# Windowed attention into a squared-ReLU MLP on one core: from a scheduler's order to the written order, with rows 0 and 1 laid out by hand

## The chip, the core and the metric

The kernel runs on one core of a Trainium2 chip. The metric is the device time of one execution in microseconds (us). The engines are TensorE (PE in the profile; PEld is its weight load), VectorE (DVE), ScalarE (ACT), GpSimd (POOL) and SyncE (SP, which here only issues DMAs).

## The reference

Attention over 8 batch rows, 8 heads, 576 positions and head size 64 is followed by a two-layer product. Heads 0 to 3 see a plain window of 32 positions, heads 4 to 7 every fourth position in a window of 128.

```
scores = matmul(q, k^T) / sqrt(64)          # (8, 8, 576, 576)
plain:   0 <= i - j < 32
dilated: 0 <= i - j < 128 and (i - j) % 4 == 0
attn = softmax(where(mask, scores, -1e9)); o = matmul(attn, v)
x = o as (4608 tokens, 512)                 # token = row * 576 + position
out = (max(x @ w_in, 0) ** 2) @ w_out       # w_in (512, 2048), w_out (2048, 512)
```

## The kernel before

The kernel works in fp16 with fp32 sums. A row is one batch index. The 4608 tokens are also cut into nine chunks of 512 for the two products. Chunk c needs rows up to c, so chunk b-1 is worked beside the attention of row b.

**Loads.** SP issues the loads of sliding q and k into `sq` (L83), of v into `sv` in six pieces (L92) and of dilated v into `sd` in two (L97, L98). These three buffers exist once. POOL issues the casting loads: dilated q and k into `nd` (L105), `w_in` into `wi` in three pieces (L110), `w_out` into `wo` in four quarters (L117). Stores of the output go out on SP too (L232). A row loads 1.18 MB into `sq`, 0.75 into `sv`, 0.82 into `sd` and 0.59 into `nd`.

**Casts.** `cast_sliding_qk` makes `nq` from `sq` in four pieces, two of q and two of k: in row 0 on ACT (q) and DVE (k), later on POOL. `cast_v_sliding` and `cast_v_dilated` make `vp` and `vd` from `sv` and `sd` on POOL.

**Attention of a row.** PE transposes q and k into PSUM (`pt`, `pd`), and DVE and ACT copy them to `QKTp` and `QKTd`. PE forms score tiles (`ps`, `pz`), ACT takes their exponential into `AT` (L288), DVE multiplies by the 0/1 mask (L289). PE forms values and row sums (`pav`, `paw`), DVE normalizes them into `x` (L330, L331), PE transposes them back (`px`, `py`), and DVE copies that into `xT` (L380, L398), which is the input of the first product. All these PSUM tiles share a pool of two buffers of two banks, `papool`: each tile waits until the one two places earlier has been read out.

**The two products of a chunk** are a generator, `moe_gen`. For each of 16 `ffc`, four matmuls sum `ph` (L205), ACT applies the ReLU into `rt` (L215; three buffers), and DVE squares it into `g` (L216). Then for each of four token tiles `t`, 16 matmuls sum `po` (L221), ACT copies it to `ot` (L231; three buffers), and SP stores it. `ph` and `po` share a pool of four PSUM buffers, `pmool`. One step of the generator is two matmuls. `pump(n)` takes n steps, and `attn` calls it with a `gap` between the steps of attention.

**Who sets the order.** The kernel is written in one sequence, and the framework's scheduler then orders each engine's instructions by priority, moving ready work ahead of what was written before it. So the built order isn't the written one. Three one-column writes to `sq`, `sv` and `sd` (L451 to L453) stand in the source after the first product's beginning, but on DVE they are built into row 0's opening, ahead of the masks and inside the mask multiplications. Row 1's loads depend on them and are issued right behind row 0's. In row 1 and later the second score tile of a pair (`ps_0_1`) was placed two `ph` matmuls behind the first (`ps_0_0`).

Of the kernel before, what the change touches and what calls it, by code (L numbers as in the profile page):

```python
# [8 lines left out]
FP16 = mybir.dt.float16  # L9
# [4 lines left out]
P = 128  # L14
# [3 lines left out]
def kernel(  # L18
# [43 lines left out]
    pmool = ctx.enter_context(tc.tile_pool(name="pmool", bufs=4, space=bass.MemoryType.PSUM))  # L62


    xT = const.tile([P, NDM, NTOK], FP16, name="xT")
    wi = wpool.tile([P, NDM, DFF], FP16, name="wi")
    wo = wpool.tile([P, NFF, DM], FP16, name="wo")
# [29 lines left out]
        nc.sync.dma_start(out=sd[PADD:P, 0, :, :], in_=vv[0:QD])  # L97
        nc.sync.dma_start(out=sd[:, 1, :, :], in_=vv[QD - PADD : CL])  # L98

    def load_dilated_qk(b):  # L100
        nd = natp.tile([QB, 2, 2, 12 * D], FP16, name=f"nd{b}", tag="nd")
        for i, src in enumerate((q, k)):
            s4 = src[b, HH:H].rearrange("(g e) (p j) d -> e p g (j d)", e=2, j=12)
            for e in range(2):
                nc.gpsimd.dma_start(out=nd[48 * e : 48 * (e + 1), i, :, :], in_=s4[e])  # L105
        return nd

    def load_w_in():
        for f0, f1 in ((0, 512), (512, 1024), (1024, 2048)):
            nc.gpsimd.dma_start(  # L110
                out=wi[:, :, f0:f1],
                in_=moe_w_in[:, f0:f1].rearrange("(dh dl) f -> dl dh f", dl=P),
            )
# [17 lines left out]
    def cast_sliding_qk(b, engs):  # L131
        n = natp.tile([QB, 2, 6, HH, D], FP16, name=f"nq{b}", tag="nq")
        for i in range(2):
            for half in range(2):
                j0 = 3 * half
                copy(
                    engs[i],
                    n[:, i, j0 : j0 + 3, :, :],
                    sq[:, i, :, D * j0 : D * (j0 + 3)].rearrange("p h (j d) -> p j h d", d=D),
                )  # L140
        return n

    def cast_v_sliding():
        for m in range(0, NB, 2):
            nc.gpsimd.tensor_copy(vp[:, m : m + 2, :, 0:D], sv[:, m : m + 2, :, :])  # L145
# [8 lines left out]


    load_sliding_qk(0)
    nds = {0: load_dilated_qk(0)}
    nc.vector.memset(sv[0:PADP, 0, :, :], 0.0)
    nc.vector.memset(sd[0:64, 0, :, :], 0.0)
    load_v(0)  # L160
# [2 lines left out]
    nc.scalar.activation(warm, warm, ACTF.Exp)  # L163

    make_identity(nc, ident)
    reli = const.tile([P, QB], I16, name="reli")
    nc.gpsimd.iota(reli, pattern=[[1, QB]], base=0, channel_multiplier=-1)
    relf = const.tile([P, QB], FP32, name="relf")
    nc.vector.tensor_copy(relf, reli)
    lo_ = const.tile([P, QB], FP16, name="lo_")  # L170
# [26 lines left out]
    )  # L197


    def moe_gen(c):  # L200
        g = gp.tile([P, NFF, TOKC], FP16, name=f"g{c}", tag="g")
        for ffc in range(NFF):
            ph = pmool.tile([P, TOKC], FP32, name=f"ph{c}_{ffc}", tag="pm")
            for dmk in range(NDM):
                nc.tensor.matmul(  # L205
                    ph,
                    wi[:, dmk, ffc * P : ffc * P + P],
                    xT[:, dmk, c * TOKC : (c + 1) * TOKC],
                    start=(dmk == 0),
                    stop=(dmk == NDM - 1),  # L210
                )
                if dmk == 1:
                    yield
            rt = osb.tile([P, TOKC], FP16, name=f"rt{c}_{ffc}", tag="rt")
            nc.scalar.activation(rt, ph[:], ACTF.Relu)  # L215
            nc.vector.tensor_mul(g[:, ffc, :], rt, rt)  # L216
            yield
        for t in range(TOKC // P):
            po = pmool.tile([P, DM], FP32, name=f"po{c}_{t}", tag="pm")
            for ffc in range(NFF):  # L220
                nc.tensor.matmul(  # L221
                    po,
                    g[:, ffc, t * P : (t + 1) * P],
                    wo[:, ffc, :],
                    start=(ffc == 0),
                    stop=(ffc == NFF - 1),
                )
                if ffc % 2 == 1 and ffc < NFF - 1:
                    yield
            ot = osb.tile([P, DM], FP32, name=f"ot{c}_{t}", tag="ot")  # L230
            nc.scalar.copy(ot, po)  # L231
            nc.sync.dma_start(  # L232
                out=out[(c * 4 + t) * P : (c * 4 + t + 1) * P, :], in_=ot
            )
            yield

    pending: list = []

    def pump(n):
        for _ in range(n):  # L240
            while pending:
                try:
                    next(pending[0])
                    break
                except StopIteration:
                    pending.pop(0)
# [5 lines left out]
    def t_sliding(b, n, hp):  # L252
        pt = pa(f"pt{b}_{hp}", FP16)
        for i in (1, 0):
            for j in range(6):
                nc.tensor.transpose(  # L256
                    pt[:, i, QB * j : QB * (j + 1)],
                    n[:, i, j, 2 * hp : 2 * hp + 2, :],
                    ident[0:QB, 0:QB],
                )  # L260
        for i, eng in ((1, nc.vector), (0, nc.scalar)):
            copy(
                eng,
                QKTp[:, i, hp, PADP:].rearrange("x (p j) -> x p j", j=6),
                pt[:, i, 0:UW].rearrange("x (j p) -> x p j", j=6),
            )
# [101 lines left out]
    def x_sliding(b, half, xs):  # L368
        px = pa(f"px{b}_{half}", FP16)
        for m3 in range(3):  # L370
            m = 3 * half + m3
            x = xs[m // 2][:, m % 2].rearrange("p h d -> p (h d)")
            for c in range(2):
                nc.tensor.transpose(
                    px[:, 0, 288 * c + QB * m3 : 288 * c + QB * (m3 + 1)],
                    x[:, P * c : P * (c + 1)],
                    ident[0:QB, 0:QB],
                )
        t0 = b * S + 288 * half
        nc.vector.tensor_copy(  # L380
            xT[:, 0:2, t0 : t0 + 288],
            px[:, 0, 0:UW].rearrange("x (c t) -> x c t", c=2),
        )

    def x_dilated(b, t, xs):
        py = pa(f"py{b}_{t}", FP16)
        for a in range(2):
            for e in range(2):
                x = xs[a][:, e].rearrange("p h d -> p (h d)")
                for c in range(2):  # L390
                    o = 288 * c + QD * (2 * a + e)
                    nc.tensor.transpose(  # L392
                        py[:, 0, o : o + QD],
                        x[0:QD, P * c : P * (c + 1)],
                        ident[0:QD, 0:QD],
                    )
        t0 = b * S + 288 * t
        nc.vector.tensor_copy(  # L398
            xT[:, 2:4, t0 : t0 + 288].rearrange("x c (i r) -> x c i r", r=DIL),
            py[:, 0, 0:UW].rearrange("x (c r i) -> x c i r", c=2, r=DIL),  # L400
        )

    def attn(b, nq, nd, gap):
        t_sliding(b, nq, 0)
        pump(gap)
        t_sliding(b, nq, 1)
        pump(gap)
        t_dilated(b, nd, 0)
        pump(gap)
        s_sliding(b, 0)  # L410
        pump(gap)
        t_dilated(b, nd, 1)
        pump(gap)
        s_sliding(b, 1)
        pump(gap + 2)
        s_dilated(b, 0)
        pump(gap + 2)
        s_dilated(b, 1)
        pump(gap + 1)
        xs = []  # L420
        for mp in range(3):
            xs.append(av_sliding(b, mp))
            pump(gap)
            if mp == 1:
                x_sliding(b, 0, xs)
                pump(gap)
        ys = []
        for a in range(2):
            ys.append(av_dilated(b, 0, a))
            pump(gap)  # L430
        x_sliding(b, 1, xs)
        pump(gap)
        zs = []
        for a in range(2):
            zs.append(av_dilated(b, 1, a))
            pump(gap)
        x_dilated(b, 0, ys)
        pump(gap)
        x_dilated(b, 1, zs)

    nq = cast_sliding_qk(0, (nc.scalar, nc.vector))
    cast_v_sliding()
    load_w_in()
    cast_v_dilated()
    load_w_out()
    attn(0, nq, nds[0], 0)
    pending.append(moe_gen(0))
    pump(1)
    pump(14)

    nc.vector.memset(sq[:, :, :, 0:1], 0.0)  # L451
    nc.vector.memset(sv[:, 1, :, 0:1], 0.0)
    nc.vector.memset(sd[:, 1, :, 0:1], 0.0)  # L453
    load_sliding_qk(1)
    load_v(1)
    nds[1] = load_dilated_qk(1)
    pump(18)
    for b in range(1, B):
        if b > 1:
            pending.append(moe_gen(b - 1))  # L460
            pump(1)
        nq = cast_sliding_qk(b, (nc.gpsimd, nc.gpsimd))
        cast_v_sliding()
        cast_v_dilated()
        if b + 1 < B:
            load_sliding_qk(b + 1)
            load_v(b + 1)
            nds[b + 1] = load_dilated_qk(b + 1)
        attn(b, nq, nds[b], 1 if b == 1 else 3)
        pump(1000)  # L470
    for c in range(B - 1, NTOKC):
        pending.append(moe_gen(c))
# [31 lines left out]
```

## Time and profile before

| | |
|---|---|
| times of three runs | 356.32, 1806.59, 355.76 us; median 356.32 |
| profiled execution | 355.09 us, span of its trace 353.3 us, TensorE clock 0.99 |
| busy in the span | PE 318.3, DVE 192.2, ACT 158.9, POOL 83.2 us |
| matmuls L205 and L221 | 576 each, 64 in a row take 13.8 us |
| DMA | 40.81 MB moved |

The span runs from the first instruction to the last; the profiled execution's own time is 1.8 us longer. PE's busy time counts modelled ends of pipelined matmuls, so single matmuls look longer (0.38 us) than their pitch (0.216 us). Idle time of an engine other than PE costs nothing by itself; it matters where PE waits for it.

### The profile page before, as it was taken

The numbers are of one execution on the slowest core, as the hardware profiler recorded it, in microseconds if no ns is written. First come the engines' busy times: TensorE is split into PE (matmuls) and PEld (weight loads), VectorE is DVE, ScalarE is ACT, GpSimd is POOL, SyncE is SP. The second block draws the span as 40 slices with busy tenths as digits, with TensorE's granted clock in tenths as the row PEclk, the third lists the DMA queues.
The fourth block names the chain that finished last, engine by engine and source line by source line (L and its number), as shares of the span: only waits on it lengthen the run. The fifth ranks groups of instructions, "written<-read, shape, count | busy, mean of one in ns | idle before, by whom it ended". The sixth has DMA issues, their size and how long they took to land.

```text
span 353.3 us, 6704 instructions
## 1 busy us (share of the span) xinstructions
PE 318.3 (90%) x2656; PEld 164.3 (46%) x2656; DVE 192.2 (54%) x422; ACT 158.9 (45%) x296; POOL 83.2 (24%) x130
## 2 busy tenths in 40 slices
PE   0468875996999999999999999999999999999995
PEld 0355332553455545554555455545554554444442
DVE  2676951764874576557655775577557653402400
ACT  3250641605931594149414941494149415614611
POOL 3471527057252322232223222002200000000000
PEclk9999996999999999999999999999999999999999
DMA  8999999959994482448243424300110011011011
GB/s 183 224 211 202 208 254 194 207 131 258 248 196 129 141 170 58 129 128 188 58 125 118 67 58 129 115 2 3 61 60 0 2 68 52 0 61 59 1 61 60
DMA packets 49840, 40.81 MB, mean 116 GB/s; under 512 B 26000, under 2 KB 44688, under 8 KB 49808
## 3 DMA queue, kind: packets, MB, share of 16 engines
q1 hardware_dynamic: 42528, 31.46, 35.1%
q0 software_dynamic: 7280, 8.92, 15.0%
q8 instruction: 21, 0.34, 0.4%
q14 instruction: 11, 0.09, 0.1%
HBM read 39.85 MB, written 9.44 MB: 139 GB/s over the span
## 4 chain that ended last, share of the span: by engine, by line
PE 61%; DMA 16%; ACT 7%; DVE 6%; issue 4%; POOL 2%; SPq 2%; POOLq 0%; ACTq 0%
PE po L221 31%; PE ph L205 22%; DMA sq<-in_k_dram 5%; DMA wi<-in_moe_w_in_dram 4%; DMA sq<-in_q_dram 3%; ACT rt L215 3%; DVE QKTd L129 3%; DVE g L216 2%; DMA sv<-in_v_dram 2%; SPq L92 2%; PE paw L359 2%; DMA out_dram<-ot 2%; ACT QKTd L127 1%; PE pt L256 1%; POOL nq L129 1%
## 5 line engine op out<-in xcount | busy, mean ns | idle before, releaser
L205 PE MATMUL ph<-xT,wi 128*128 128x512 f16 x576 | 139.1, 382 | 2.3 <-ACT rt L215 1.0
L221 PE MATMUL po<-wo,g 128*128 128x512 f16 x576 | 140.1, 381 | 0.0
L215 ACT ACTIVATE rt<-ph 128x512 f16<-128x512 f32 x144 | 84.9, 608 | 36.2 <-PE ph L205 32.8
L216 DVE TENSOR_TENSOR g<-rt 128x512 f16<-128x512 f16 x144 | 68.7, 480 | 58.5 <-ACT rt L215 56.0
L205 PEld LDWEIGHTS <-wi 128*128 128x128 f16 x576 | 51.6, 98 | 57.5 <-issue 3.7
L231 ACT COPY ot<-po 128x512 f32<-128x512 f32 x36 | 21.1, 586 | 121.4 <-PE po L221 110.7
L221 PEld LDWEIGHTS <-g 128*128 128x128 f16 x576 | 51.4, 98 | 50.2 <-issue 0.6
L129 POOL CAST nq<-sq 96x768 f16<-96x768 f32 x28 | 24.1, 894 | 43.3 <-PE pt L256 20.7
L145 POOL CAST vp<-sv 128x512 f16<-128x512 f32 x24 | 16.3, 682 | 74.3 <-PE pav L345 35.3
L150 POOL CAST vd<-sd 128x512 f16<-128x512 f32 x32 | 19.5, 624 | 32.9 <-PE paw L359 25.6
L288 ACT ACTIVATE AT<-ps 128x576 f16<-128x576 f32 x32 | 19.8, 671 | 11.2 <-PE ps L298 11.2
L331 DVE TENSOR_TENSOR x_d<-paw,rcp_d 72x512 f16<-72x512 f32 x32 | 22.0, 686 | 1.1
L272 PE MATMUL pd<-ident,nd 96*128 96x96 f16 x192 | 12.1, 219 | 10.2 <-DMA nd<-in_k_dram 6.8
L256 PE MATMUL pt<-ident,nq 96*128 96x96 f16 x192 | 11.7, 215 | 10.1 <-DVE nq L129 9.6
L129 DVE COPY QKTp<-pt 128x576 f16<-128x576 f16 x16 | 12.0, 756 | 14.1 <-PE pt L256 14.1
L288 ACT ACTIVATE AT<-pz 128x576 f16<-128x576 f32 x32 | 19.1, 650 | 0.1
L289 DVE TENSOR_TENSOR AT<-AT,maskp 128x576 f16<-128x576 f16 x32 | 15.0, 468 | 7.5 <-ACT AT L288 5.1
L129 DVE COPY QKTd<-pd 128x288 f16<-128x288 f16 x32 | 13.0, 448 | 9.2 <-PE pd L272 9.1
L272 PEld LDWEIGHTS <-nd 96*128 96x128 f16 x192 | 11.1, 105 | 14.0 <-issue 10.9
L398 DVE COPY xT<-py 128x576 f16<-128x576 f16 x16 | 12.1, 757 | 9.9 <-PE py L392 9.9
L256 PEld LDWEIGHTS <-nq 96*128 96x128 f16 x192 | 10.6, 103 | 13.6 <-DVE nq L129 9.6
L289 DVE TENSOR_TENSOR AT<-AT,maskd 128x576 f16<-128x576 f16 x32 | 15.1, 474 | 3.2 <-ACT AT L288 0.3
(51 smaller groups left out, 194.5 us busy)
## 6 DMA issues: line engine op xcount, KB each, us to landing
out_dram<-ot SPq DMA_DIRECT2D x36, 256.0 KB, 2.4
sv<-in_v_dram SPq DMA_DIRECT2D x40, 128.0 KB, 4.4
sq<-in_q_dram SPq DMA_DIRECT2D x8, 576.0 KB, 10.5
sq<-in_k_dram SPq DMA_DIRECT2D x8, 576.0 KB
sd<-in_v_dram SPq DMA_DIRECT2D x8, 512.0 KB
nd<-in_q_dram POOLq DMA_DIRECT2D x16, 144.0 KB, 5.8
nd<-in_k_dram POOLq DMA_DIRECT2D x16, 144.0 KB, 6.0
sd<-in_v_dram SPq DMA_DIRECT2D x8, 288.0 KB
```

Source lines behind the costliest of these rows:

```text
L129: eng.tensor_copy(o, i)
L150: nc.gpsimd.tensor_copy(vd[:, t, c : c + 2, :, 0:D], sd[:, t, :, D * c : D * (c + 2)].rearrange("p h (c d) -> p c h d", d=D),)
L205: nc.tensor.matmul(ph, wi[:, dmk, ffc * P : ffc * P + P], xT[:, dmk, c * TOKC : (c + 1) * TOKC], start=(dmk == 0), stop=(dmk == NDM - 1),)
L215: nc.scalar.activation(rt, ph[:], ACTF.Relu)
L216: nc.vector.tensor_mul(g[:, ffc, :], rt, rt)
L221: nc.tensor.matmul(po, g[:, ffc, t * P : (t + 1) * P], wo[:, ffc, :], start=(ffc == 0), stop=(ffc == NFF - 1),)
L231: nc.scalar.copy(ot, po)
L256: nc.tensor.transpose(pt[:, i, QB * j : QB * (j + 1)], n[:, i, j, 2 * hp : 2 * hp + 2, :], ident[0:QB, 0:QB],)
L272: nc.tensor.transpose(pt[:, i, QB * j : QB * (j + 1)], n[:, i, g, P * j : P * (j + 1)], ident[0:QB, 0:QB],)
L288: nc.scalar.activation(AT[:, u, 0:UW], ps[:, :, 0 : UW // 2], ACTF.Exp, scale=scale)
L289: nc.vector.tensor_mul(AT[:, u, 0:UW], AT[:, u, 0:UW], mask)
L331: nc.vector.tensor_tensor(out=x[0:w], in0=pv[:, :, :, 0:D], in1=rcp[0:w].unsqueeze(3).to_broadcast([w, 2, HH, D]), op=ALU.mult,)
```

## The change

The kernel enters `tc.manual_schedule()`, and from there each engine follows the order in which the code is written. The code is laid out anew for it:

- Row 0: the index pattern `reli` is made on POOL ahead of the `nd` loads; the masks come ahead of the k cast on DVE; q is cast by ACT, the first half of k by DVE, the second by POOL; `w_in` is issued after that cast and ahead of the v casts. Attention of row 0 stands alone, without products between its steps.
- The first product of chunk 0 follows. After three of its 16 `ffc`, DVE writes one column of `sq` and of row 1's `nd` buffer; row 1's `sq` and `nd` loads depend on these writes, and `w_out` is issued after them. `sv` and `sd` of row 1 are written and loaded after row 1's first transposes.
- The second product of chunk 0 goes by quarters of `w_out`, with four `po` sums open at a time (`mm2_by_rows_gen`). Row 1's attention is laid between its steps.
- `xT` copies (L380, L398) are on ACT in all rows.
- In rows 2 to 7 `pav_2` comes ahead of `px_0`, and gaps are 3 and 4 steps in the scores, and 3 in the values (2 in row 2, which begins with 12 steps of the first product).

In the order built from it, each engine has the same kinds of instructions as before, apart from the 32 `xT` copies that went from DVE to ACT, a second one-column write, and the k cast of row 0. In a later row DVE's sequence is now first `QKTp` copy, `g_0`, `g_1`, second `QKTp` copy, `g_2`, `QKTd` copies, `g_3`; before it was first `QKTp` copy, `g_0`, second `QKTp` copy, `g_1`, `g_2`, `QKTd` copies, `g_3`. ACT's is now first `QKTp` copy, `rt_0`, `rt_1`, second `QKTp` copy, `rt_2`, `QKTd` copies, `rt_3`; before it was `rt_0`, first `QKTp` copy, `rt_1`, second `QKTp` copy, `rt_2`, `rt_3`, `QKTd` copies. `ps_0_1` follows `ps_0_0` on PE directly.

```diff
+    ctx.enter_context(tc.manual_schedule())
...
     load_sliding_qk(0)
-    nds = {0: load_dilated_qk(0)}
+    reli = const.tile([P, QB], I16, name="reli")
+    nc.gpsimd.iota(reli, pattern=[[1, QB]], base=0, channel_multiplier=-1)
+    nds = {0: dilated_buffer(0)}
+    load_dilated_qk(0, nds[0])
...
+    def mm2_by_rows_gen(c, g):
+
+        pos = [
+            pmool.tile([P, DM], FP32, name=f"po{c}_{t}", tag="pm") for t in range(TOKC // P)
+        ]
+        for f4 in range(0, NFF, 4):
+            for t, po in enumerate(pos):
+                for ffc in range(f4, f4 + 4):
+                    mm2(c, g, po, t, ffc)
+                    if ffc % 2 == 1 and ffc < NFF - 1:
+                        yield
+                if f4 + 4 == NFF:
+                    store(c, t, po)
+                    yield
...
-        nc.vector.tensor_copy(
+        nc.scalar.copy(
             xT[:, 0:2, t0 : t0 + 288],
...
-        nc.vector.tensor_copy(
+        nc.scalar.copy(
             xT[:, 2:4, t0 : t0 + 288].rearrange("x c (i r) -> x c i r", r=DIL),
...
-    nq = cast_sliding_qk(0, (nc.scalar, nc.vector))
+    nq = cast_sliding_qk(0, (nc.scalar, nc.scalar, nc.vector, nc.gpsimd))
+    load_w_in()
     cast_v_sliding()
-    load_w_in()
     cast_v_dilated()
+    attn_scores(0, nq, nds[0], (0, 0))
+    attn_values(0, 0)
+    g0 = hidden(0)
+    pending.append(mm1_gen(0, g0))
+    pump(6)
+    nds[1] = dilated_buffer(1)
+    nc.vector.memset(sq[:, :, :, 0:1], 0.0)
+    nc.vector.memset(nds[1][:, :, :, 0:1], 0.0)
+    load_sliding_qk(1)
+    load_dilated_qk(1, nds[1])
     load_w_out()
-    attn(0, nq, nds[0], 0)
-    pending.append(moe_gen(0))
-    pump(1)
-    pump(14)
-
-    nc.vector.memset(sq[:, :, :, 0:1], 0.0)
+    nq = cast_sliding_qk(1, (nc.gpsimd,) * 4)
+    pump(26)
+    pending.append(mm2_by_rows_gen(0, g0))
+    t_sliding(1, nq, 0)
     nc.vector.memset(sv[:, 1, :, 0:1], 0.0)
     nc.vector.memset(sd[:, 1, :, 0:1], 0.0)
-    load_sliding_qk(1)
     load_v(1)
-    nds[1] = load_dilated_qk(1)
-    pump(18)
-    for b in range(1, B):
-        if b > 1:
-            pending.append(moe_gen(b - 1))
-            pump(1)
-        nq = cast_sliding_qk(b, (nc.gpsimd, nc.gpsimd))
+    cast_v_sliding()
+    cast_v_dilated()
+    load_sliding_qk(2)
+    load_v(2)
+    nds[2] = dilated_buffer(2)
+    load_dilated_qk(2, nds[2])
+    pump(2)
+    attn_scores(1, nq, nds[1], (2, 2), begun=True)
+    attn_values(1, 1)
+    pump(1000)
+    for b in range(2, B):
+        pending.append(moe_gen(b - 1))
+        pump(12 if b == 2 else 1)
+        nq = cast_sliding_qk(b, (nc.gpsimd,) * 4)
...
-        attn(b, nq, nds[b], 1 if b == 1 else 3)
+        attn_scores(b, nq, nds[b], (3, 4))
+        attn_values(b, 2 if b == 2 else 3)
         pump(1000)
```

## The prediction

> **What bounds the kernel now.** I read the page's busy times first, then the table by stretches cut at row boundaries, then the timeline of the two stretches where TensorE (PE) stands still, then one steady row engine by engine.
>
> ```profile
> PE 318.3 (90%) x2656; PEld 164.3 (46%) x2656; DVE 192.2 (54%) x422; ACT 158.9 (45%) x296; POOL 83.2 (24%) x130
> ...
> q1 hardware_dynamic: 42528, 31.46, 35.1%
> q0 software_dynamic: 7280, 8.92, 15.0%
> ```
>
> PE is the bound. The queues give prices: q1 took 0.351 x 353.3 = 124 us for 31.46 MB, 3.9 us per MB; the casting queue q0 took 53 us for 8.92 MB, 5.9 us per MB.
>
> ```profile
> 0.00:30.00 30.00, 12.82 (x170) 9.92 (x171) 17.28 (x49) 10.28 (x18) 14.12 (x27) 1.00 1.06 205
> 30.00:47.76 17.76, 16.38 (x87) 7.50 (x85) 13.37 (x21) 8.20 (x15) 6.46 (x9) 1.00 1.18 214
> 47.76:78.03 30.27, 23.42 (x253) 12.11 (x252) 15.27 (x34) 9.53 (x18) 11.36 (x18) 0.89 0.98 187
> 78.03:116.34 38.31, 35.45 (x317) 18.31 (x316) 22.83 (x48) 17.58 (x34) 16.30 (x25) 1.00 0.89 216
> 116.34:223.30 106.96, 104.89 (x949) 54.90 (x948) 66.55 (x144) 53.37 (x102) 30.56 (x45) 1.00 0.46 114
> 223.30:293.60 70.30, 69.88 (x633) 36.57 (x632) 43.24 (x96) 35.57 (x68) 4.46 (x7) 1.00 0.09 33
> 293.60:353.30 59.70, 55.47 (x257) 24.95 (x255) 13.61 (x32) 24.40 (x41) 0.00 (x0) 1.00 0.11 40
> ```
>
> Second column is length, then PE busy. Row 0's attention and the first product of chunk 0 end at 47.76. Row 1 with the second product of chunk 0 takes 30.27, row 2 38.31. Rows 3 to 5 take 106.96 / 3 = 35.65 each, rows 6 and 7 35.15, the last two chunks without attention 59.70. The DMA share is about 1 up to 116 us, so loads are scarce only there.
>
> ```profile
> 12.90 0.19 DVE L173 TENSOR_SCALAR lo__124<-relf 128x72 f16<-128x72 f32 x1 [1.47 <-DMA sv<-in_v_dram]
> 13.61 1.42 DVE L129 COPY QKTp<-pt 128x576 f16<-128x576 f16 x2
> 15.08 1.12 PE L272 MATMUL pd<-ident,nd 96*128 96x96 f16 x12 [2.72 <-ACT QKTp L127]
> 57.31 1.12 PE L272 MATMUL pd<-ident,nd 96*128 96x96 f16 x12 [6.85 <-DMA nd<-in_k_dram]
> 82.13 0.59 ACT L231 COPY ot<-po 128x512 f32<-128x512 f32 x1 [7.37 <-DMA out_dram<-ot]
> ```
>
> The brackets are the idle time before. In row 0 a one-column `sv` write, pulled ahead to DVE's start, waits for a load and holds the masks, `QKTp` and PE. In row 1 PE waits 6.85 for `nd`, queued behind `w_out`. In row 2 the fourth `ot` copy waits for the first store, which the SP queue holds behind loads.
>
> ```profile
> 225.89 0.61 ACT L215 ACTIVATE rt<-ph 128x512 f16<-128x512 f32 x1
> 227.05 0.64 ACT L127 COPY QKTp<-pt 128x576 f16<-128x576 f16 x1 [0.54 <-DVE QKTp L129]
> 226.26 0.76 DVE L129 COPY QKTp<-pt 128x576 f16<-128x576 f16 x1 [0.32 <-PE pt L256]
> 228.56 0.81 DVE L129 COPY QKTd<-pd 128x288 f16<-128x288 f16 x2
> 229.41 0.70 ACT L127 COPY QKTd<-pd 128x288 f16<-128x288 f16 x2 [0.25 <-DVE QKTd L129]
> 230.16 0.30 PE L298 MATMUL ps<-QKTp 64*128 64x96 f16 x6
> ```
>
> This is row 6. `ps_0_1` needs the PSUM buffer of `pd_0`, which is free when ACT has copied `QKTd`; it starts 230.16 - 223.30 = 6.86 after the row began, and two `ph` matmuls fill part of the wait. A row spends only about a microsecond waiting.
>
> [...]
>
> ```profile
> 35.81 5.80 DVE L216 TENSOR_TENSOR g<-rt 128x512 f16<-128x512 f16 x4 [1.31 <-ACT rt L215]
> ...
> 36.61 3.13 POOL L129 CAST nq<-sq 96x768 f16<-96x768 f32 x4
> ```
>
> Four `g` products take 5.80 beside four casts; one alone takes 0.43. [...]
>
> **The change, part by part.** The order of instructions now is the written one on every engine.
>
> Row 0. The masks come before the k cast, the one-column writes later. The k halves go to DVE and POOL[...]. Transposes end at 11.3 as now; `QKTp` is copied 11.4 to 12.2 by DVE, to 12.8 by ACT, and `pd_0` starts at 12.9 instead of 15.08: -2.2. Then ACT copies `QKTd` before `exp`, where `exp` now fits into its wait for DVE: about +0.6 for each of two groups, +1.2. From the first `pav` DVE is the chain: seven normalizations of 0.88; four `xT` copies (0.46, 0.44, 0.76, 0.76 = 2.4) leave it for ACT, half of that returned by two more PSUM waits: -1.2 to -2. The last `xT` lands near 32 instead of 34.5. The current order has eight `ph` matmuls done before that point, the new one two: 62 x 0.216 (64 take 13.81) = 13.4. The first product ends at 45.4: -2.4. `w_in` is issued near 10.5 instead of 15.7 and needs 2.1 MB x 5.9 = 12.5 us behind row 0's remaining loads, so by about 28: hidden.
>
> Row 1 loads. `sq` and `nd` wait for a DVE write behind `g_2`, so near 35.5; DMA idles some 7 us before. `sq` costs 1.18 MB x 3.9 = 4.6, `nd` 0.59 x 5.9 = 3.5, the first `w_out` quarter 3.1, the queues sharing. Queued behind on POOL are `w_out` and the `nq` casts. k lands near 44.5 (bounds 43, as row 0's took 7.4, to 47, the longest shown being 11.6). Two casts of 0.83 follow: PE waits about 1.3. The first `w_out` quarter lands near 47.7: 0.8 more. `sv` and `sd` follow `pt_0`; with the rest of `w_out` they take 15.5 / 1.1 = 14 us, so by 62, when the `paw` matmuls want them: 0, at worst 4.
>
> Row 1 itself: 64 matmuls 13.8, attention's PE work 6.8 (a steady row less 27.65 of big matmuls and its waits), waits inside attention 1.9, loads 2.1: 24.6, against 30.27: -5.7. The 6.85 stall is gone; what is late next is the chain of attention itself, because only 13.8 us of matmuls lie between its steps.
>
> `w_out` by quarters: same 64 matmuls; it needs all four PSUM buffers, so the four `ot` copies come within 3 us at the end and three `ot` buffers hold them. The fourth waits for the first store, which SP issues only after row 2's loads (10.6 us of q1 beside `nd`): landing near 75, PE out of buffers at about 72.6. Wait 3.2 (bounds 0 and 5.5, the store's landing shown now).
>
> Steady rows. DVE now does `g_1` before the second `QKTp` copy, ACT does the first `QKTp` copy before `rt_0`, and `ps_0_1` follows `ps_0_0` with nothing between. From the row's first matmul: `pt_0` ends 0.95, ACT `QKTp` 1.94 to 2.57, `rt_0` 2.44, `rt_1` 2.94 to 3.54, `g_1` 3.57, DVE `QKTp` 3.93 to 4.69 (2.96 in row 6 now), ACT to 5.36, `rt_2` to 5.85, `g_2`, DVE `QKTd` 6.22 to 7.03, ACT to 7.77. `ps_0_1` starts at 7.82; PE was ready at 6.19: 1.63 of waiting. The second pair repeats it through `rt_5`, `g_5`: `ps_1_1` at 12.3, ready at 11.41: 0.89. Held against row 6 at the same count of matmuls PE is 1.8 later, and nothing later in the row gives it back. So 36.9; where POOL casts (rows 3 to 6) another 0.4, near the 0.5 by which such rows differ now: 37.3. Rows 3 to 7: 4 x 37.3 + 36.9 = 186.1 against 177.3: +8.8. Row 2: 27.65 + 6.8 + 2.5 + 3.2 = 40.2 against 38.31: +1.9.
>
> `xT` on ACT: 28 more copies of some 0.65 after row 0, ACT at about 51%, behind no PE wait; if that cover failed, 0.65 per copy at most. Tail: unchanged.
>
> Sum: 45.4 + 24.6 + 40.2 + 186.1 + 59.7 = 356.0, against 353.3. The profiled execution took 355.09, 1.8 above its span: 357.8. The median shown, 356.32, is 1.2 above that; with half of it I say **358.5**.
>
> **Rivals.** (1) The start gains and steady rows stay as they are, because the hardware's slack absorbs the late copies: 358.5 - 8.8 - 1.4 (row 2's share) = 348.3. For it: ACT and DVE are half idle. Against it: the chain above is built of measured durations and FIFO order. (2) Slower: holding row 1's loads back starves row 1. DMA, already at share 1, lies idle from about 28 to 35.5, and the rest of rows 1's and 2's loads with `w_out` must fit behind it. Should k land at 47 and `sd` past 66, `pt_0` costs 2.5 more, the `paw` matmuls 4, the store wait 1.5: 366.5. It decides from a `sq` landing time above 10 us. For it: landings of 9.5 to 11.6 now under load. Against: `sq` starts on idle queues. (3) That the order would not change is excluded by the built program's order.
>
> **How the numbers follow.** Forecast 0.65, rival 1 0.13, rival 2 0.22. The forecast's own spread (steady row 36.3 to 37.6, load waits 0 to 4, store wait 0 to 5.5) is 353 to 364. Two per cent, about what a measurement of this kernel can tell from no change, is 7.1 us: 349.2 and 363.4. Faster 0.10, same 0.65, slower 0.25. Range 350 to 367.
>
> **What would show it.** Right: `pd_0` of row 0 near 12.9; the first product ending near 45; row 1 ended near 70 with no wait on `nd`; rows 3 to 7 at 37, `ps` waiting on ACT `QKTd` over 1 us each. Wrong: steady rows at 35.7 (then faster), or PE waiting more than 4 us in row 1 for `sq`, `sd` or `wo` (then slower).

## The result and the profile after

The changed kernel took 374.25 us (median; 373.6 to 376.8) against 356.32: a ratio of 1.051, 95% interval [1.040, 1.062]. The prediction was 358.5 with a range up to 367; the result lies outside it, on the slower side. One run of the kernel before took 1806.59 us, and two profiled executions below (four `ot` buffers alone, 369.49 us; without the holding writes, 368.49 us) were longer than the other runs of their kernels, so medians are compared, and from those two profiles only waits and order are read.

The profiled execution took 376.8 us, its span 375.0. The sum in the prediction was made for a span: 356.0. So 19.0 us are to be explained; the median run, with a span of 372.5, would leave 16.5.

Page of the changed kernel, busy times:

```profile
PE 321.9 (86%) x2656; PEld 166.8 (44%) x2656; DVE 174.9 (47%) x390; ACT 179.1 (48%) x328; POOL 85.6 (23%) x131
```

The same 2656 matmuls as before: TensorE (PE) is only 3.6 us busier, so most of the time lost against the kernel before is PE waiting. The table by stretches (length, then busy time of PE, PEld, DVE, ACT, POOL; clock; DMA share; GB/s), cut at the row boundaries:

```profile
0.00:32.29 32.29, 14.10 (x188) 11.28 (x189) 17.50 (x46) 12.26 (x21) 10.49 (x22) 1.00 0.85 169
32.29:48.83 16.54, 16.43 (x68) 6.71 (x66) 7.53 (x17) 9.71 (x18) 7.91 (x12) 1.00 0.61 124
48.83:74.53 25.70, 22.24 (x252) 11.84 (x253) 13.78 (x32) 11.91 (x22) 10.09 (x16) 1.00 1.20 208
74.53:121.45 46.92, 36.85 (x317) 18.94 (x316) 19.62 (x44) 20.25 (x38) 16.40 (x27) 0.93 0.68 146
121.45:161.73 40.28, 36.32 (x318) 18.88 (x317) 21.14 (x44) 20.35 (x38) 10.77 (x15) 0.96 0.52 111
161.73:199.98 38.25, 34.74 (x317) 18.45 (x316) 20.75 (x44) 19.95 (x38) 10.60 (x15) 1.00 0.54 117
278.39:315.57 37.18, 34.75 (x317) 18.45 (x316) 19.20 (x44) 19.95 (x38) 0.00 (x0) 1.00 0.08 30
315.57:375.00 59.43, 55.42 (x257) 24.95 (x255) 13.60 (x32) 24.40 (x41) 0.00 (x0) 1.00 0.11 41
```

Rows 3 and 4 and row 7 are shown; rows 5 and 6 took 39.86 and 38.55. Set beside the prediction:

| stretch | before | predicted | after | excess over predicted |
|---|---|---|---|---|
| first product of chunk 0 ends | 47.76 | 45.4 | 48.83 | +3.4 |
| row 1 | 30.27 | 24.6 | 25.70 | +1.1 |
| row 2 | 38.31 | 40.2 | 46.92 | +6.7 |
| rows 3 to 7 | 177.26 | 186.1 | 194.12 | +8.0 |
| tail | 59.70 | 59.7 | 59.43 | -0.3 |

The excesses sum to 18.9. Where they are is seen in the timeline. First the early stalls (start, length, engine, line, operation; in brackets the idle time before and its releaser):

```profile
12.32 1.12 PE L305 MATMUL pd<-ident,nd 96*128 96x96 f16 x12 [0.56 <-ACT QKTp L131]
...
34.26 0.60 ACT L219 ACTIVATE rt<-ph 128x512 f16<-128x512 f32 x1 [1.10 <-PE ph L209]
35.97 0.60 ACT L219 ACTIVATE rt<-ph 128x512 f16<-128x512 f32 x1 [1.11 <-PE ph L209]
37.54 0.60 ACT L219 ACTIVATE rt<-ph 128x512 f16<-128x512 f32 x1 [0.97 <-PE ph L209]
38.40 0.60 ACT L219 ACTIVATE rt<-ph 128x512 f16<-128x512 f32 x1 [0.27 <-PE ph L209]
38.54 0.07 DVE L491 MEMSET sq<- 96x8 f32 x1
...
49.79 0.56 PE L289 MATMUL pt<-ident,nq 96*128 96x96 f16 x9 [0.66 <-POOL nq L133]
51.42 0.81 PE L224 MATMUL po<-wo,g 128*128 128x512 f16 x3 [1.08 <-DMA wo<-in_moe_w_out_dram]
57.15 0.68 PE L305 MATMUL pd<-ident,nd 96*128 96x96 f16 x12
...
75.60 9.18 SPq L235 DMA_DIRECT2D out_dram<-ot  x4
83.83 0.59 ACT L234 COPY ot<-po 128x512 f32<-128x512 f32 x1 [9.38 <-DMA out_dram<-ot]
84.47 4.69 PE L209 MATMUL ph<-xT,wi 128*128 128x512 f16 x12 [7.18 <-ACT ot L234]
```

Row 0's opening and row 1's waits are near what was predicted. Two things are not. The first `rt` activations are 1.71 us apart instead of 0.86: four `ph` matmuls took 0.427 us each, half speed, from 32.3 to about 37. And in row 2 PE waited 7.18 us for `ot`, then ran twelve matmuls in 4.69 us, mostly at half speed again (the twelve at 74.53, at full speed, took 2.75).

The half speed at the start was not new at 32.3. Twelve transposes (`pd`) took 1.12 us in row 0, at 12.32, and 0.68 in row 1, at 57.15; six score matmuls (`ps`) 0.42 and 0.30, eight `pav` 0.60 and 0.42. In the kernel before the same twelve `pd` took 1.12 both in row 0 and at 57.31, and six `ps` 0.42 at 59.21, where its trace shows a granted clock of 0.50 (53.87 to 60.70). So by the times of equal matmuls PE was at half speed in row 0 and until about 37. The column of the clock doesn't show it: the record of the clock begins at 37.24 us in this trace and at 33.39 in that of the kernel before, each time at full speed, and where there is no record the column says 1.00. So at the start the time of equal matmuls is to be read, not the column.

Then the later rows: row 3 (with GpSimd's `nq` casts) and row 7 (without).

```profile
129.34 0.30 PE L331 MATMUL ps<-QKTp 64*128 64x96 f16 x6 [1.63 <-ACT QKTd L131]
129.45 1.79 POOL L133 CAST nq<-sq 96x768 f16<-96x768 f32 x2 [9.29 <-DMA sq<-in_q_dram]
129.83 1.69 DVE L220 TENSOR_TENSOR g<-rt 128x512 f16<-128x512 f16 x2 [1.32 <-ACT rt L219]
131.47 2.10 POOL L133 CAST nq<-sq 96x768 f16<-96x768 f32 x2 [0.23 <-DMA sq<-in_k_dram]
132.80 1.04 DVE L220 TENSOR_TENSOR g<-rt 128x512 f16<-128x512 f16 x1
135.41 0.30 PE L331 MATMUL ps<-QKTp 64*128 64x96 f16 x6 [2.32 <-ACT QKTd L131]
135.65 2.65 PE L209 MATMUL ph<-xT,wi 128*128 128x512 f16 x7
...
286.29 0.30 PE L331 MATMUL ps<-QKTp 64*128 64x96 f16 x6 [1.63 <-ACT QKTd L131]
286.77 0.92 DVE L220 TENSOR_TENSOR g<-rt 128x512 f16<-128x512 f16 x2 [1.32 <-ACT rt L219]
290.83 0.30 PE L331 MATMUL ps<-QKTp 64*128 64x96 f16 x6 [0.80 <-ACT QKTd L131]
```

The first score wait is 1.63 in both, the number of the prediction. The second is 0.80 in row 7 (0.89 was predicted) but 2.32 in row 3, where two `g` took 1.69 us instead of 0.92 beside the casts. After that wait seven matmuls took 2.65 us where a run of 0.216 each, with the modelled end of the last, makes 1.7. The clock was granted at half three times in this execution: from 81.61 to 88.44 (store wait), 136.22 to 139.63 (row 3) and 214.73 to 218.14 (row 5). Stretches ahead of the two later ones, and two in row 6, which kept the full clock:

```profile
132.81:136.22 3.41, 1.09 (x16) 0.68 (x16) 2.09 (x5) 1.56 (x5) 0.76 (x1) 1.00 0.97 234
136.22:139.63 3.41, 3.41 (x24) 1.23 (x22) 2.10 (x6) 2.58 (x6) 0.00 (x0) 0.50 0.07 24
211.31:214.73 3.42, 1.52 (x18) 0.90 (x18) 2.03 (x5) 1.96 (x5) 0.37 (x1) 1.00 1.11 202
214.73:218.14 3.41, 3.41 (x24) 1.23 (x23) 2.42 (x6) 2.96 (x6) 0.00 (x0) 0.50 0.17 53
248.86:252.27 3.41, 2.62 (x27) 1.33 (x25) 3.41 (x5) 1.39 (x3) 2.76 (x3) 1.00 1.04 209
252.27:255.69 3.42, 2.04 (x14) 0.95 (x14) 1.85 (x5) 2.79 (x7) 0.00 (x0) 1.00 0.78 186
```

The three half-speed stretches were 6.83, 3.41 and 3.41 us long. The last two came after the long waits of rows 3 and 5 (2.32 us up to 135.41, 1.90 up to 213.52); in the 3.41 us ahead of them PE was busy for only 1.09 and 1.52 us. Row 6 had a wait of 2.17 us (up to 253.65) and kept the clock at 1.00; PE was busy for 2.62 and 2.04 us in the two stretches around that wait. So in this execution the length of a wait alone doesn't tell whether half speed follows: 1.90 us was followed by it and 2.17 us was not.

### The profile page after: what moved, and what is told of

Read it like the earlier page. It is cut to its first block, busy times and chain, and to the rows that moved or that the text cites. A ratio compares the mean times of both kernels' runs of the same rounds, so it can differ in the third digit from the quotient of the medians.

```text
span 375.0 us, 6727 instructions
## 1 busy us (share of the span) xinstructions
PE 321.9 (86%) x2656; PEld 166.8 (44%) x2656; DVE 174.9 (47%) x390; ACT 179.1 (48%) x328; POOL 85.6 (23%) x131
## 3 DMA queue, kind: packets, MB, share of 16 engines
q1 hardware_dynamic: 42528, 31.46, 35.5%
## 4 chain that ended last, share of the span: by engine, by line
PE 63%; DMA 12%; DVE 10%; ACT 7%; SPq 3%; issue 2%; POOL 1%; ACTq 0%; POOLq 0%
PE po L224 31%; PE ph L209 24%; DVE g L220 4%; DMA sd<-in_v_dram 4%; DMA sq<-in_k_dram 3%; ACT rt L219 3%; DMA wo<-in_moe_w_out_dram 3%; SPq L95 3%; DVE QKTd L133 2%; DMA out_dram<-ot 2%; PE paw L392 2%; DVE QKTp L133 2%; ACT QKTd L131 2%; ACT QKTp L131 2%; DVE AT L322 1%
## 5 line engine op out<-in xcount | busy, mean ns | idle before, releaser
L209 PE MATMUL ph<-xT,wi 128*128 128x512 f16 x576 | 142.6, 394 | 7.2 <-ACT ot L234 7.2
L209 PEld LDWEIGHTS <-wi 128*128 128x128 f16 x576 | 53.9, 100 | 68.2 <-issue 16.0
L149 POOL CAST vp<-sv 128x512 f16<-128x512 f32 x24 | 16.5, 689 | 78.2 <-issue 38.2
L331 PE MATMUL ps<-QKTp 64*128 64x96 f16 x192 | 10.2, 213 | 24.3 <-ACT QKTd L131 24.3
L154 POOL CAST vd<-sd 128x512 f16<-128x512 f32 x32 | 19.4, 616 | 42.3 <-PE paw L392 31.6
L413 ACT COPY xT<-px 128x576 f16<-128x576 f16 x16 | 10.2, 639 | 38.7 <-PE px L407 38.7
L131 ACT COPY QKTd<-pd 128x288 f16<-128x288 f16 x32 | 11.2, 402 | 25.9 <-DVE QKTd L133 21.4
L363 DVE RECIPROCAL rcp_d<-paw 72x8 f32<-72x8 f32 x32 | 6.5, 202 | 34.9 <-PE paw L392 34.9
L431 ACT COPY xT<-py 128x576 f16<-128x576 f16 x16 | 10.2, 640 | 22.6 <-PE py L425 22.5
L331 PEld LDWEIGHTS <-QKTp 64*128 64x128 f16 x192 | 6.7, 96 | 31.6 <-issue 23.8
L322 DVE TENSOR_TENSOR AT<-AT,maskp 128x576 f16<-128x576 f16 x32 | 17.1, 541 | 7.8 <-ACT AT L321 6.1
L131 ACT COPY QKTp<-pt 128x576 f16<-128x576 f16 x16 | 10.2, 639 | 21.6 <-DVE QKTp L133 19.7
```

Of the source, the lines that this page charges most:

```text
L131: nc.scalar.copy(o, i)
L154: nc.gpsimd.tensor_copy(vd[:, t, c : c + 2, :, 0:D], sd[:, t, :, D * c : D * (c + 2)].rearrange("p h (c d) -> p c h d", d=D),)
L209: nc.tensor.matmul(ph, wi[:, dmk, ffc * P : ffc * P + P], xT[:, dmk, c * TOKC : (c + 1) * TOKC], start=(dmk == 0), stop=(dmk == NDM - 1),)
L322: nc.vector.tensor_mul(AT[:, u, 0:UW], AT[:, u, 0:UW], mask)
L331: nc.tensor.matmul(ps[:, e, QB * m3 : QB * (m3 + 1)], QKTp[r, 1, hp, QB * m : QB * m + P], QKTp[r, 0, hp, PADP + QB * m : PADP + QB * (m + ...
```

## The experiments

The ratio of each is to the kernel before, run on the same chip; its medians there were 355.0 to 356.0. A sequence of row lengths in this section is from one first transpose (`pt`) to the next: rows 3 to 6 of the changed kernel are 40.28, 38.25, 39.86, 38.55 by this measure, of the kernel before 35.65, 35.65, 35.65, 35.18.

**The written order or the new layout?** Two halves of the change. The new source under the scheduler:

```diff
-    ctx.enter_context(tc.manual_schedule())
```

> The changed source without the manual schedule: the framework's scheduler orders the engines again, everything else as changed. Theory A (the written order of later rows costs, through ACT and DVE copies that stand behind rt and g): rows 3 to 7 fall from 194.1 us back to about 178, so some 356 to 360 us in all. Theory B (the hand layout itself, holding row 1's loads back, costs): the time stays within 5 us of 374.

It took 363.28 us, 1.022 [1.017, 1.026]. Rows 3 to 6 are 35.66, 35.64, 35.65, 35.17: the excess of the later rows is gone to the last tenth. The whole is above the 356 to 360 of theory A, because row 3 begins only at 124.53 us (before: 116.78, after: 121.88); in row 2 the store wait is longer still:

```profile
90.26 3.57 PE L208 MATMUL ph<-xT,wi 128*128 128x512 f16 x8 [10.89 <-ACT ot L233]
```

So the order costs the later rows, and the layout of the loads and stores costs something else. The other half is the source of before under the written order:

```diff
+    ctx.enter_context(tc.manual_schedule())
```

> The kernel before with one line added: every engine follows the written order, and nothing is laid out anew. Theory A (the written order costs the later rows, through two matmuls missing between the two score tiles of a pair and through casts on GpSimd): rows 3 to 7 take 37 to 38.5 us instead of 35.5, and the row's first score pair waits 1 us or more on the ACT copy of QKTd; with row 0 laid out for a scheduler the early part loses as well: 365 to 380. Rival (the new layout costs, not the order; the order alone is neutral): 356 to 360 with rows at 35.5.

It took 372.56 us, 1.047 [1.040, 1.055], which is nearly the whole loss of the change. Its stretches of rows 2 to 4:

```profile
79.23:117.25 38.02, 34.92 (x317) 18.49 (x316) 22.76 (x48) 17.57 (x35) 10.51 (x15) 1.00 0.52 116
117.25:155.94 38.69, 34.92 (x318) 18.47 (x317) 23.50 (x48) 17.57 (x35) 10.46 (x15) 1.00 0.52 115
155.94:196.18 40.24, 36.48 (x317) 18.91 (x316) 23.46 (x48) 17.88 (x35) 10.75 (x15) 0.96 0.52 110
```

Row 3 begins at 117.25, near the 116.78 of before: little is lost by then. The loss is in the later rows: rows 3 to 6 take 158.4 us together instead of 142.1, each 38.6 to 40.8, as in the changed kernel. `xT` is copied by DVE in this kernel, so its move to ACT isn't the cause.

**The store wait.** `ot` gets a pool of its own with four buffers, so that the fourth copy needs no landed store.

```diff
+    otp = ctx.enter_context(tc.tile_pool(name="otp", bufs=4))
...
-        ot = osb.tile([P, DM], FP32, name=f"ot{c}_{t}", tag="ot")
+        ot = otp.tile([P, DM], FP32, name=f"ot{c}_{t}", tag="ot")
```

> The changed kernel with four ot buffers instead of three. Theory C (row 2's 7.18 us of PE idle is the fourth ot copy waiting for the first store): that idle goes, and with it the half-clock stretch behind it (12 matmuls in 4.53 us, 1.9 more than at full clock), so 7 to 9 us less: about 366. Rival: the stores are late because DMA is full, the wait comes back at the next ot or at the loads of row 2, and the gain is under 3 us.

364.39 us, 1.022 [1.017, 1.027], so 10 us less than the change. PE has no wait on `ot` in row 2; in the changed kernel that wait was 7.18 us and the half speed behind it cost 1.9 more. How the 10 us divide isn't fully shown: the three other runs were granted a mean clock of 0.990 to 0.995, against 0.982 in the changed kernel, so they met less half speed elsewhere too. The same edit to the kernel before:

> The kernel before with four ot buffers of their own and nothing else. If its 7.37 us wait of ScalarE for an ot buffer in row 2 holds TensorE: 353 to 354, 1 to 3 us less. If not (TensorE was on loads there): 355 to 356, no difference. It tells how much of the four buffers' gain after the change repairs something that the change itself made.

353.97 us, 0.997 [0.995, 0.999]: about 1 us, where PE waited 0.95 for the same `ot`. So some 9 of the 10 us repair what the change itself brought.

**Who makes the store late?** Row 1's `sq` and `nd` loads and `w_out` are issued right behind row 0's casts, without the writes that hold them; `sv` and `sd` stay held.

```diff
     cast_v_dilated()
+    nds[1] = dilated_buffer(1)
+    load_sliding_qk(1)
+    load_dilated_qk(1, nds[1])
+    load_w_out()
     attn_scores(0, nq, nds[0], (0, 0))
...
-    nds[1] = dilated_buffer(1)
-    nc.vector.memset(sq[:, :, :, 0:1], 0.0)
-    nc.vector.memset(nds[1][:, :, :, 0:1], 0.0)
-    load_sliding_qk(1)
-    load_dilated_qk(1, nds[1])
-    load_w_out()
```

> The changed kernel without the holding writes: row 1's sq and nd loads and w_out are issued right behind row 0's casts, and the first column of sq and nd isn't rewritten before them. Theory F (holding back is harmless or useful: row 1's transposes wait under 1 us and its values 1.1 us, and early loads compete with row 0's): row 1 keeps its 25.7 us and loses at most 1.5 us of waits, w_in may come later; 372.5 to 376. Rival (my prediction's second rival: holding back leaves the queues idle for 10 us and pushes rows 1 and 2's loads and the first store late): the store wait in row 2 of 7.2 us on PE shrinks by 4 us or more, and the total falls to 367 to 370.

364.91 us, 1.024 [1.017, 1.030]: 9 us less, a little more than the rival of this expectation asked for. Row 1's waits of 0.66 and 1.08 are gone, and the store wait is down from 7.18 to 2.22:

```profile
69.45 7.35 SPq L235 DMA_DIRECT2D out_dram<-ot  x4
75.87 0.58 ACT L234 COPY ot<-po 128x512 f32<-128x512 f32 x1 [4.41 <-DMA out_dram<-ot]
76.50 4.42 PE L209 MATMUL ph<-xT,wi 128*128 128x512 f16 x12 [2.22 <-ACT ot L234]
```

SP issues the stores from 69.45 on instead of 75.60, because its queue, in which row 2's loads stand ahead of them, is through earlier. So holding back row 1's loads does starve the start, only not where I had looked for it: in row 1 it cost waits of 1.7 us, in row 2 5.0. The rest of the 9 is not read from this profile; the mean clock of the other runs was 0.991 to 1.0.

**The casts on GpSimd.** In rows 2 to 7 the v casts are written ahead of the `nq` casts, so that these stand behind casts that wait for PE's values of the row in work, and no longer meet its scores.

```diff
-        nq = cast_sliding_qk(b, (nc.gpsimd,) * 4)
         cast_v_sliding()
+        nq = cast_sliding_qk(b, (nc.gpsimd,) * 4)
```

> The changed kernel with POOL's nq casts written behind the vp casts of the same row from row 2 on, so that they run in the values phase of the row before and not beside the score phase. Theory D (POOL's casts lengthen g and mask products on DVE in the score phase: 1.69 us for two g and 1.44 for two masks instead of 0.92 and 1.00): the second ps wait falls from about 2 to 0.8 us in rows 3 to 6, and the half-clock stretches of rows 3 and 5 go with it: 4 x 1.2 + 3 = about 8 us less, 366. Rival: the casts only move and lengthen the normalizations, under 2 us.

367.24 us, 1.031 [1.026, 1.036]: 7 us less. Rows 3 to 6 are 37.18, 37.19, 37.18, 37.18: alike, at the length of row 7 in the changed kernel, and at full clock (1.00 in rows 3 and 4). In row 3:

```profile
129.01 0.91 DVE L220 TENSOR_TENSOR g<-rt 128x512 f16<-128x512 f16 x2 [1.32 <-ACT rt L219]
133.08 0.30 PE L331 MATMUL ps<-QKTp 64*128 64x96 f16 x6 [0.80 <-ACT QKTd L131]
```

`g` is back at 0.91 for two, the second score wait at 0.80. The account of the changed kernel's rows closes: over row 7's 37.18 they took 3.10, 1.07, 2.68 and 1.37 us more; their second score wait was longer than 0.80 by 1.52, 1.07, 1.10 and 1.37, and half speed added 1.58 in rows 3 and 5. What remains over 35.65 is 1.5 us a row.

**The half-speed start.** The first two matmuls of `ph_0` to `ph_3` are laid between row 0's last transposes, where the scheduler had put them (`begin(b, ...)` emits them; the generator then leaves them out).

```diff
+        begin(b, 0, 1)
         x_dilated(b, 0, ys)
         pump(gap)
+        begin(b, 2)
         x_dilated(b, 1, zs)
+        begin(b, 3)
```

> The changed kernel with the first two matmuls of ph_0 to ph_3 laid between row 0's last transposes, as the scheduler had them. Theory E (TensorE starts the first dense run of 512-column matmuls at half speed for some 5 us, 0.427 us each[...]): eight matmuls fill the waits of about 0.3 us around the last transposes (-0.5 to -1) and bring the half speed stretch forward into them, so that the first product of chunk 0 ends at 46.0 to 47.3 instead of 48.83, total 371.5 to 373. Rival (half speed depends on what the matmuls wait for, or nothing is saved because the copies of xT still end at 33): the first product ends at 48.5 to 49, total 374.

372.0 us, 1.047 [1.042, 1.052], within the expectation, but by a different sum:

```profile
28.80 1.90 PE L211 MATMUL ph<-xT,wi 128*128 128x512 f16 x4
30.49 0.68 PE L440 MATMUL py<-ident,x_d 72*128 72x72 f16 x8
31.58 0.43 PE L440 MATMUL py<-ident,x_d 72*128 72x72 f16 x8
32.73 12.25 PE L211 MATMUL ph<-xT,wi 128*128 128x512 f16 x56 [0.29 <-ACT xT L446]
35.35 0.07 DVE L509 MEMSET sq<- 96x8 f32 x1
47.63 0.30 PE L304 MATMUL pt<-ident,nq 96*128 96x96 f16 x3 [2.65 <-POOL nq L133]
```

The change to full speed came earlier by about 6 us: eight `py` transposes took 0.68 us at 30.49 and 0.43 at 31.58, so by these two it lies between 30.5 and 31.6, against 37.24. The four `ph` matmuls at 28.80 still ran at half speed (1.90 us), the 56 from 32.73 on at full (12.25 us, 0.219 each). So with the eight matmuls in this place full speed was there before the last wait for `xT` (0.29 us, up to 32.73); the kernel before had them too, and eight `py` took 0.68 us there at 31.84 and 0.53 at 33.17. The product ended at 45.0, 3.9 earlier and earlier than expected, and PE then waited 2.65 for `nq`, that is for the held load of k, and ran at half speed once more (four `po` matmuls took 1.87 us at 49.28, and 1.03 at 51.87). Two faults of the change had covered each other. The write that releases row 1's loads stands behind the first matmuls of this product: it came at 35.35 instead of 38.54, and the store wait of this run is 4.02 us instead of 7.18. (The write isn't all of it: the run with the v casts first has a store wait of 4.42 with the write at 38.03.)

**The order of the copies.** A first attempt wrote `rt` and `g` of every `ph` two matmuls later and put one step of matmuls between the two score tiles.

```diff
         for half, ps in enumerate(tiles):
...
+            if half == 0:
+                pump(mid)
...
-            rt = osb.tile([P, TOKC], FP16, name=f"rt{c}_{ffc}", tag="rt")
-            nc.scalar.activation(rt, ph[:], ACTF.Relu)
-            nc.vector.tensor_mul(g[:, ffc, :], rt, rt)
+            if c == 0 or ffc == NFF - 1:
+                evict(ffc, ph)
+            else:
+                held.append((ffc, ph))
```

> The changed kernel with rt and g of each ffc written two matmuls later, and one generator step between the two ps tiles of a pair from row 2 on; PE's other order is kept. ACT and DVE then have the sequence of the kernel before. Theory A: the waits of ps for QKTd fall from 1.63 and 0.8 to 2.3 us to under 1 us each, rows 3 to 7 from 194.1 to about 180, the whole to about 360. Rival (POOL's casts and the clock, not the order, make these rows long): under 4 us gained.

369.04 us, 1.037 [1.033, 1.041]. A gain of 5 where 14 was hoped for; rows 3 to 6 are 38.55, 38.06, 38.00, 38.02, with the casts still beside the scores (the second wait is 1.76 in row 3). To see this edit without them, it was run together with the v casts first and four `ot` buffers:

> The changed kernel with four edits together: four buffers of their own for ot, rt and g written two matmuls later, one step of matmuls between the two score tiles of a pair, and GpSimd's v casts ahead of its nq casts in rows 2 to 7. If the three causes (store wait, written order of the score pair, casts beside the scores) are separate and add up: 374.25 - 9.9 - 7 - 5 x 1.2 = 351.4, rows 3 to 7 at 35.7 to 36.2. If they share time (a wait removed comes back elsewhere): 355 to 360, rows at 37. If the edit of the score pair does nothing even without the casts beside it: 357 and rows at 37.2.

361.04 us, 1.015 [1.011, 1.019], rows 37.07, 37.07, 37.06, 37.06: the third of the cases expected by its rows, 4 us above it in all. With clean casts the edit brings 0.1 us a row. In row 2 the v casts, which wait for late loads there, held `nq` up:

```profile
81.84 0.30 PE L300 MATMUL pt<-ident,nq 96*128 96x96 f16 x3 [2.96 <-POOL nq L134]
122.47 0.30 PE L342 MATMUL ps<-QKTp 64*128 64x96 f16 x6 [1.10 <-ACT QKTd L132]
```

Two matmuls between the score tiles fill 0.43 us, but `QKTd` was still late: ACT began to copy it 6.71 us into a row, against 5.68 in row 6 of the kernel before, which has no casts. With `rt_0` written two matmuls late it stood behind the first ACT `QKTp` copy, not ahead of it, and DVE reached its second `QKTp` copy at 3.02 against 2.53. DVE's order of copies is the scheduler's here too; it was late because `g_0` ahead of that copy waits for `rt_0`. The positions in PE's and DVE's order were right, in ACT's not. So a second attempt wrote the copies in exactly the scheduler's order, each `rt` and `g` between the DVE half and the ACT half of a copy (v first from row 3 on only, four `ot` buffers):

```diff
         for i, eng in ((1, nc.vector), (0, nc.scalar)):
+            if i == 0:
+                pump(mid)
+                flush()
             copy(
```

> The changed kernel in manual order, with the steady rows' copies written in the scheduler's order: in rows 2 to 7 each rt and g is written between the VectorE and the ScalarE half of a QKTp or QKTd copy, so that ScalarE does rt_0 ahead of its first QKTp copy, VectorE the second QKTp copy ahead of g_1, and ScalarE rt_3 ahead of QKTd; two matmuls lie between the two score tiles of a pair; GpSimd casts v ahead of nq from row 3 on; ot has four buffers. Against the kernel with four edits (361.0, rows 37.07) this tells whether the order of the copies is what costs a row 1.4 us. Theory A (it is): the first score wait falls from 1.10 to about 0.54, the second from 0.28 to nothing, rows 3 to 7 take 35.65, total 361.0 - 5 x 1.4 - 3 (row 2's nq no longer behind v) = 351. Rival (the order of the copies is a trifle; manual order or xT copies on ScalarE cost it): rows stay at 37.0, total 358.

346.7 us, 0.976 [0.971, 0.980]: faster than the kernel before, and better than expected. Rows 3 to 6 are 35.17, 35.18, 35.17, 35.17. Row 3 from its first `pt` at 110.35:

```profile
110.35:145.52 35.17, 34.96 (x317) 18.30 (x316) 18.95 (x44) 20.30 (x39) 9.88 (x15) 1.00 0.65 129
...
115.18 0.82 DVE L134 COPY QKTd<-pd 128x288 f16<-128x288 f16 x2
116.03 0.70 ACT L132 COPY QKTd<-pd 128x288 f16<-128x288 f16 x2 [0.25 <-DVE QKTd L134]
116.78 0.30 PE L348 MATMUL ps<-QKTp 64*128 64x96 f16 x6
```

The wait of the second score tile isn't in brackets any more: its start at 116.78 follows the ACT copy's end at 116.73. It is 6.43 us into the row, exactly as in row 6 of the kernel before (230.16, its first `pt` at 223.73). A row is now as short as before's row 6, which had no casts. Against the kernel with four edits 1.9 us a row are gained, and about 4.7 by row 3's start. In rows 3 to 5 of the two traces PE, DVE and GpSimd have the same order of instructions, and only ACT's differs, so the 1.9 are ACT's order alone.

**All together.** Early loads added to that, and then the head of the first product as well:

> As the kernel with the scheduler's order of copies, and row 1's sq and nd loads and w_out issued right behind row 0's casts, without holding writes. Theory (holding back costs by pushing all later loads and the first stores): row 3's first transposes come 2 to 5 us earlier, total 346 to 349. Rival (its gain of 9 us in the run without holding writes was the store wait alone, which four ot buffers have taken away already): equal to the kernel without it within 1 us, 351.

344.59 us, 0.969 [0.966, 0.973]: 2.1 less, though the intervals of the two overlap. With four `ot` buffers, holding back costs only row 1's waits: 1.83 and 0.47 for `nq` and 0.22 for `wo` without this edit, none of them with it.

> As the one before with the first two matmuls of ph_0 to ph_3 laid between row 0's last transposes. That edit alone took the changed kernel from 374.25 to 372.0; if it adds up here: 344 to 347, about 0.97 of the kernel before. Rival (the half speed stretch at the start has the same length wherever it begins, and w_in or v loads set the start): no gain, 347 to 351.

343.31 us, 0.966 [0.962, 0.971], 1.3 less; these intervals overlap too. Row 1 begins at 46.56 instead of 48.15. This version is 3.4% faster than the kernel before.

## Why the prediction was wrong

**Bound and steps that held.** `pd_0` of row 0 started at 12.32 (12.9 predicted). The wait on `nd` is gone, and row 1 took 25.70 (24.6 predicted). The waits in a steady row's chain of copies were right to 0.1 us: 1.63 predicted and measured for the first pair, 0.89 and 0.80 for the second, row 7 37.18 against 36.9. The experiments confirm its cause: the same source with the scheduler's order has rows of 35.65, and the written order with the copies laid in that order 35.17. `xT` on ACT cost nothing, as predicted: rows of 35.17 have it there.

**The store wait: "Wait 3.2 (bounds 0 and 5.5...)"** measured 7.18, and half-speed matmuls came on top. I had SP's queue finish its loads in time for a landing near 75. SP issued the stores only at 75.60, and the fourth `ot` copy came at 83.83. The mechanism was named; its size was wrong by more than a factor of two, and its upper bound was too low. It left out the delay that the hold-back hands down the queue, which I priced under rival 2 only, and at 1.5 us for this wait. The hold-back was also longer than planned: the releasing write came at 38.54, not near 35.5, because the matmuls ahead of it ran at half speed (0.427 us each). Rival 2's place for the harm (k, `sd`) was wrong and its mechanism right: the run with early loads shows it.

**The casts: "where POOL casts (rows 3 to 6) another 0.4"**. Rows 4 and 6, at full clock, took 1.1 and 1.4 us more than row 7. I had carried the 0.5 over from the kernel before. There the casts lengthened one `g` ahead of `QKTd` (0.90 us instead of 0.43, row 3 at 121.26), and the row is 0.5 longer. In the changed kernel they fall later in the row and meet three `g` and two mask products ahead of the second pair's `QKTd`, for which PE waits already. Two `g` took 1.69 instead of 0.92 us there. I had shown such a meeting in the first product of the kernel before, four `g` in 5.80 us beside four casts, and put no price of that size on the steady rows.

**Half speed: "62 x 0.216", and no price behind a wait.** The step priced the first product at full speed from its first matmul, and counted the eight `ph` matmuls that it took out of row 0 only as work to be done later. The trace shows a slower start. In row 0 twelve `pd` took 1.12 us, against 0.68 in row 1, and the `ph` matmuls, which begin at 32.29, took 0.427 us each until about 37.2 and 0.216 after it. The later half-speed stretches (clock 0.50, 6.83, 3.41 and 3.41 us long) came with waits of 7.18, 2.32 and 1.90 us. The lines of before had shown it as well: `pd` takes 1.12 us in row 0, and row 1 stands there with a clock of 0.89, behind the 6.85 us wait for `nd`. I passed over it and put no price of this kind on the waits that I added. It cost about 2.6 us at the start (16.43 for 64 matmuls instead of 13.8), 1.9 in row 2 (4.69 instead of 2.75), and in rows 3 and 5 PE was busy 36.32 us, 1.6 longer than the 34.74 of rows 4 and 6.

Of the 19.0 us, then, half speed is 7.7, the store wait 4.0 beyond its 3.2, and the casts 3.5 beyond their 1.6 (they lengthened the second score waits of rows 3 to 6 by 5.1). The other 3.8 are spread over the stretches, about 0.3 of it in each of rows 3 to 7.

What stays open is how little work is followed by half speed. In the later rows of the changed kernel PE was busy for 1.09 and 1.52 of 3.41 us ahead of it, and 1.94 and 2.04 us of 3.42 in rows 4 (from 173.76 us) and 6 (from 252.27) were not followed by it. More than these four figures is not shown. With the v casts first, the clock was 1.00 in rows 3 and 4 (PE busy 34.74 and 34.75 us), and rows 5 and 6 have the same length.

## What to carry to other kernels

A written order is no loss in itself: with each engine's copies in the right order a row takes 35.17 us, as the scheduler's row without casts. That kernel was 2.4% faster than the one before, but it also has four `ot` buffers, the new layout of the start and the casts moved out of the scores, and most of its gain (6.4 us) was there when row 3 began. The scheduler was not given all of these edits, so that the written order beats it is not shown. The order must be right on every engine: PE's and DVE's alone brought 0.1 us a row, with ACT's 1.9 more.

When a change brings a wait for PE or takes dense matmuls away from a sparse stretch, price the matmuls that may run at half speed behind it: here 1.9 us after the wait of 7.18, and 2.6 in the first product. When a change holds loads back, follow the queue to its last entry, the stores, and not only to the first consumer. A price seen under one order, as the casts' 0.5 us, holds for the instructions that they met there.

## What was not expected of the hardware

- By the times of equal matmuls TensorE ran row 0's transposes, scores and values at half speed (`pd` 1.12 us against 0.68 in row 1, `ps` 0.42 against 0.30, `pav` 0.60 against 0.42); in the changed kernel full speed came at 37.24, 4.95 us after the first of the 512-column matmuls. Eight of these laid among the last small ones, from 28.80 us on, moved the change from 37.24 to between 30.5 and 31.6 (eight `py` took 0.68 us at 30.49 and 0.43 at 31.58). The clock column showed 1.00 throughout, because the record of the clock begins only at 37.24.
- In the changed kernel waits of 2.32 and 1.90 us were followed by 3.41 us at a clock of 0.50 each, and one of 2.17 us was not.
- Four casts on GpSimd took 3.13 us beside the values (v casts first, row 3) and 3.9 (1.79 + 2.10) beside the scores, and DVE's `g` 0.91 and 1.69 for two: both took longer where they met. In the kernel before the loss was VectorE's: a single `g` took 3.82 us (36.30 to 40.12) beside four casts of 0.83 us each.
